# Causal attention and two feed-forward layers on one core: 128 stationary columns for every first score chunk, a minimum that moves rows to the other half of the partitions, and a new order of all operations

## The chip, the cores and the metric

One core of a Trainium2 chip runs the whole program in one launch. The metric is device time in microseconds of one execution, from the runs' times. Three runs of the kernel before took 589.15, 589.16 and 590.04 us, a median of 589.16 us. The profile is of one more execution: it took 589.2 us, of which 587.4 us lie between its first and its last instruction (the span). The other 1.8 us lie around the span. All positions below are microseconds from the span's start.

## The reference, cut to what matters

```
q, k, v: (2, 12, 448, 64) float32; scores = q @ k.T / 8, masked above the diagonal with -1e9
attn = exp(scores - max); attn = attn / (sum(attn) + 1e-9); x = attn @ v        # 24 heads
x -> (896, 768)                                       # tokens by 12 heads * 64
g = x @ w_gate; x = (g * sigmoid(g) * (x @ w_val)) @ w_out                      # d_ff 1536
h = x @ w_in; r = max(h, 0); out = (r * r) @ w_out2                             # d_ff 2048
```

The weights arrive as 64-bit floats. The kernel takes each weight tile as pairs of 32-bit words and splits it into two fp32r parts (whi, wlo). The activations are split in the same way (hi, lo), and each product is made of three matmuls.

## The kernel before

**The two stages.** The attention runs first, for 12 pairs of heads (p = 0 to 11; heads 2p and 2p+1). The feed-forward layers follow, a long row of matmuls in a fixed order (`products`, L880 and L1057). While the attention runs, the first two weight units are split (jobs J, L589 to L620), and one early product of the first unit (L880, tile early) fills two gaps near the end.

**One pair of heads, job by job.** Each job has a letter in the planner.

- LD loads q, k and v (SyncE's queue; for pair 0 also ScalarE's).
- AT turns q or k with four matmuls against the identity (L734). AC copies the result to SBUF (L740 on VectorE, L742 on ScalarE).
- S makes the scores of row chunk i of both heads (`score_mm`, L758). A head has 448 rows: chunk 0 has 64 rows and 64 columns, chunks 1, 2 and 3 have 128 rows and 192, 320 and 448 columns. The two heads lie on partitions 0 to 63 and 64 to 127 of the operand, so that two matmuls run side by side, in the two row halves of the array. Before, chunk 0 of the two heads is one 128x64 tile: each head's matmul has 64 stationary columns, and the second head's result is written to partitions 64 to 127 of the same PSUM bank.
- M takes the scaled and masked scores out of PSUM with VectorE and keeps each row's minimum (`score_max`, L775). E is the exponential with its sum (L781, ScalarE).
- RA adds 1e-9 to the sums (L786), R inverts them (L791, VectorE), N scales the rows (`normalise`, L808 or, on ScalarE, L806), NT moves 64 rows to the other partition half (`normalise_tail`, also through `scale_by`).
- T turns the probabilities, 8 matmuls for a head in two groups (L823 to L833). H copies a group out of PSUM (L843 VectorE, L845 ScalarE). V multiplies with the values, for a pair (L852). XH and XL split the result (L863, L868).

**What sets the order.** `attention_plan` gives every job an engine, a cost in ns, the jobs it waits for and the buffers it takes. `Plan.run` is a list scheduler: of all jobs that can start it takes the one that starts earliest, and among equals the one with the lowest rank (RANK plus a table FIRST with one entry per job). The jobs are then written out in that order, and each engine runs its own jobs in exactly that order. Tables in OPT choose the engine of each AC ("acd"), RA ("rad"), N ("n"), NT ("nt") and H ("h"). Where the plan sees TensorE idle in the first 24 us, `bank` writes idle matmuls (L522, `keep_warm`) into the gap; they run whether the gap is there or not. PSUM has 8 banks, taken in turn; a pair's scores take 4.

Of the kernel before, what the change touches and what calls it, by code (L numbers as in the profile page):

```python
# [10 lines left out]
F32 = mybir.dt.float32  # L11
# [342 lines left out]
def act_cost(n, sbuf=False, extra=0):  # L354
    return 76 + 0.833 * n + 43 * sbuf + 93 * extra
# [751 lines left out]
```

## Time and profile before

| | kernel before |
|---|---|
| median of 3 runs | 589.16 us (589.15 to 590.04) |
| profiled execution, its span | 589.2 us, 587.4 us |
| granted TensorE clock over the span | 1.000 |
| TensorE busy | 581.0 us (99%) |
| VectorE, ScalarE, GpSimd busy | 467.6, 283.9, 44.9 us |
| chain that ended last, by engine | PE 87%, DVE 4%, ACT 3%, DMA 2%, POOL 1% |

The engines are PE (TensorE's matmuls), PEld (its weight loads), DVE (VectorE), ACT (ScalarE), POOL (GpSimd) and SP (SyncE, which issues most DMAs). A line number is one of the kernel before. Matmuls are pipelined, so the records of neighbouring matmuls overlap, and a busy PE need not be a full one: what a group of matmuls costs is read from its start to the start of the next group.

### The profile page before, as it was taken

Reading aid. Unit: us, or ns where it says so; the run is one execution under the profiler, and the core shown is the slowest. Engines: PE = TensorE matmul, PEld = TensorE weight load, DVE = VectorE, ACT = ScalarE, POOL = GpSimd, SP = SyncE. Lnnn points to the kernel's source line nnn. Section 1 sums busy time; section 2 is a strip of 40 time slices with the busy share of each in tenths; the row PEclk is TensorE's granted clock in tenths of the full one; section 3 lists DMA queues with packets and bytes.
Section 4 is the critical chain, followed back from the end, with each engine's and each line's share of the span. In section 5 each row is a group of like instructions: output and inputs, shape, how many; then the busy total and the mean of one; then the engine's idle time right before and its main releaser. Section 6 shows DMA issues by size and latency. Waiting matters only on the chain.

```text
span 587.4 us, 8665 instructions
## 1 busy us (share of the span) xinstructions
PE 581.0 (99%) x3234; PEld 525.9 (90%) x3235; DVE 467.6 (80%) x851; ACT 283.9 (48%) x541; POOL 44.9 (8%) x119
## 2 busy tenths in 40 slices
PE   8999999999999999999999999999999999999997
PEld 4766678999999999999999999999999999999997
DVE  4998895998888888888777777888888897649741
ACT  5999895443333333332333335777777732223201
POOL 2555640000000000000000000000000000000000
PEclk9999999999999999999999999999999999999999
DMA  8775140343333333333333332333334343345102
GB/s 171 182 165 127 33 137 26 112 156 108 108 108 108 108 107 108 108 107 109 108 112 110 110 115 92 109 107 108 109 109 112 107 153 112 107 148 161 55 1 94
DMA packets 80777, 65.04 MB, mean 111 GB/s; under 512 B 34912, under 2 KB 76640, under 8 KB 80736
## 3 DMA queue, kind: packets, MB, share of 16 engines
q1 hardware_dynamic: 79808, 64.27, 37.1%
q8 instruction: 25, 0.41, 0.3%
q10 hardware_dynamic: 928, 0.23, 0.2%
q14 instruction: 16, 0.13, 0.1%
HBM read 61.73 MB, written 2.75 MB: 110 GB/s over the span
## 4 chain that ended last, share of the span: by engine, by line
PE 87%; DVE 4%; ACT 3%; DMA 2%; POOL 1%; SPq 1%; issue 1%; ACTq 0%; POOLq 0%
PE o L1057 20%; PE h L880 20%; PE v L880 15%; PE y L880 15%; PE g L880 14%; ACT P L781 2%; PE s L758 2%; POOL P L808 1%; DMA raw<-in_k_dram 1%; DVE P L775 1%; PE x L852 1%; DMA wraw<-in_moe_w_gate_dram 1%; DVE P L808 1%; DVE pt L843 1%; SPq L719 1%
## 5 line engine op out<-in xcount | busy, mean ns | idle before, releaser
L607 ACT ACTIVATE whi<-wa 128x768 fp32r<-128x768 f32 x68 | 57.4, 844 | 123.3 <-DVE wa L601 80.8
L1057 PE MATMUL o<-whi,b 128*128 128x384 f32 x336 | 85.5, 334 | 0.0
L880 PE MATMUL y<-b,whi 128*128 128x480 f32 (+1 forms) x288 | 69.2, 362 | 0.0
L589 ACT ACTIVATE wa<-wraw 128x768 f32<-128x768 f32 x68 | 61.7, 908 | 11.5 <-DVE wlo L620 11.1
L880 PE MATMUL h<-b,whi 128*128 128x480 f32 (+1 forms) x256 | 66.7, 362 | 0.0
L617 DVE TENSOR_TENSOR wa<-wa,whi 128x768 f32<-128x768 f32 x68 | 64.6, 950 | 0.4 <-ACT whi L607 0.4
L601 DVE SCALAR_TENSOR_TENSOR wa<-wraw,wa 128x768 uint32<-128x768 uint32 x68 | 64.7, 952 | 0.0
L614 DVE SCALAR_TENSOR_TENSOR wr<-wraw,wr 128x768 f32<-128x768 uint32 x68 | 64.7, 951 | 0.1
L620 DVE TENSOR_TENSOR wlo<-wa,wr 128x768 fp32r<-128x768 f32 x68 | 64.5, 949 | 0.1
L592 DVE TENSOR_SCALAR wa<-wa 128x768 f32<-128x768 f32 x68 | 38.0, 559 | 32.7 <-ACT wa L589 32.7
L1057 PEld LDWEIGHTS o<-whi,b 128*128 128x128 f32 x336 | 60.7, 188 | 0.0
L880 PEld LDWEIGHTS y<-b,whi 128*128 128x128 f32 x288 | 53.9, 187 | 3.7
L1057 PE MATMUL o<-wlo,b 128*128 128x384 f32 x168 | 56.1, 334 | 0.0
L880 PE MATMUL h<-b,wlo 128*128 128x480 f32 x192 | 53.9, 362 | 0.0
L880 PEld LDWEIGHTS h<-b,whi 128*128 128x128 f32 x256 | 48.0, 187 | 3.2
L967 ACT ACTIVATE b<-u 128x480 fp32r<-128x480 f32 (+2 forms) x24 | 13.9, 580 | 69.0 <-DVE u L963 69.0
L781 ACT ACTIVATE P<-P,st 128x448 f32<-128x448 f32 (+3 forms) x84 | 43.7, 523 | 3.1 <-DVE st L775 2.6
L880 PE MATMUL v<-ahi,whi 128*128 128x480 f32 (+2 forms) x144 | 40.4, 362 | 0.0
L880 PE MATMUL v<-alo,whi 128*128 128x480 f32 (+2 forms) x144 | 40.4, 362 | 0.0
L880 PE MATMUL v<-ahi,wlo 128*128 128x480 f32 (+2 forms) x144 | 40.4, 362 | 0.0
L880 PE MATMUL y<-b,wlo 128*128 128x480 f32 (+1 forms) x144 | 40.4, 362 | 0.0
L610 DVE TENSOR_SCALAR wr<-wa 128x768 uint32<-128x768 uint32 x68 | 38.0, 558 | 1.8
(94 smaller groups left out, 1041.4 us busy)
## 6 DMA issues: line engine op xcount, KB each, us to landing
wraw<-in_moe_w_out_dram SPq DMA_DIRECT2D x28, 768.0 KB, 4.4
wraw<-in_moe_w_in_dram SPq DMA_DIRECT2D x16, 768.0 KB, 4.7
wraw<-in_moe_w_gate_dram SPq DMA_DIRECT2D x12, 768.0 KB, 4.3
wraw<-in_moe_w_val_dram SPq DMA_DIRECT2D x12, 768.0 KB, 4.3
out_dram<-osb SPq DMA_DIRECT2D x14, 192.0 KB, 1.9
raw<-in_q_dram SPq DMA_DIRECT2D x23, 112.0 KB, 2.8
raw<-in_k_dram SPq DMA_DIRECT2D x23, 112.0 KB, 3.0
v<-in_v_dram SPq DMA_DIRECT2D x24, 96.0 KB, 2.6
```

Source lines behind the costliest of these rows:

```text
L589: nc.scalar.activation(out=af, in_=high.bitcast(F32), func=AF.Abs)
L592: engine.tensor_scalar(out=af, in0=af, scalar1=W_TINY, scalar2=W_HUGE, op0=ALU.max, op1=ALU.min)
L601: nc.vector.scalar_tensor_tensor(out=a, in0=high, scalar=0xC0000000, in1=a, op0=ALU.bitwise_and, op1=ALU.bitwise_or)
L607: nc.scalar.activation(out=split_t[n][0], in_=af, func=AF.Copy)
L610: nc.vector.tensor_scalar(out=r[0], in0=a, scalar1=0xFF800000, scalar2=None, op0=ALU.bitwise_and)
L614: nc.vector.scalar_tensor_tensor(out=rf, in0=low, scalar=2.0 ** -52, in1=rf, op0=ALU.mult, op1=ALU.mult)
L617: engine.tensor_tensor(out=af, in0=af, in1=split_t[n][0].bitcast(F32), op=ALU.subtract)
L620: engine.tensor_tensor(out=split_t[n][1], in0=af, in1=r[0].bitcast(F32), op=ALU.add)
L781: nc.scalar.activation(out=a, in_=a, func=AF.Exp, scale=-1.0, bias=st(0), accum_out=st(1))
L880: nc.tensor.matmul(out=pss[z][:, :cols], lhsT=w[p == 2][:, c], rhs=xs[k][p == 1][:, at:at + cols], start=first and k == 0 and p == 0, stop ...
L967: nc.scalar.activation(out=g_hi[m][:, at(c)], in_=up[z][:, :c[1]], func=AF.Copy)
L1057: nc.tensor.matmul(out=pss[t][:, :N], lhsT=a[f][:, tk], rhs=w[:, c], start=f + n == 0, stop=f == KF2 - 1 and n == 2)
```

## The change

Chunk 0 of the second head now takes 128 stationary columns, like every other chunk, and goes to a PSUM bank of its own. Only the first 64 rows of the result are used. Each head has an M job of its own for chunk 0 (64x64): the second head's reads PSUM partitions 0 to 63 and writes SBUF partitions 64 to 127, so that the exponential can still take both heads in one instruction. That one now waits for two M jobs. The second mask tile is gone. The planner's costs are new, FIRST is a new and shorter table, and a weight job on DVE with two tensor inputs now holds GpSimd in the plan. Nearly all engine choices go back to one default: AC on ACT, RA and N on POOL, NT on DVE, H group 0 on ACT and group 1 on DVE.

```diff
 FIRST = {
-    ('AC', 0, 0): -907.75, ('AC', 0, 1): 3963.19, ('AC', 1, 0): 2864.38, ('AC', 1, 1): -1686.58,
...
+    ('AC', 0, 0): 2.15, ('AC', 0, 1): 2.15, ('AC', 1, 0): 2.15, ('AC', 1, 1): 23.63,
...
-    "acd": ((0, 0), (2, 0), (5, 0), (11, 0), (11, 1)),
+    "acd": (),
-    "rad": (3, 5, 19, 20, 21, 22),
-    "pack": 1,
+    "rad": (),
+    "pack": 2,
...
+        (1, 3): 'D', (17, 2): 'D', (21, 2): 'D',
...
+            if k[0] == "J" and engine == "DVE" and k[2] in (3, 6, 7, 8):
+                free["Pool"] = max(free.get("Pool", 0), start) + cost
...
-    return 76 + 0.833 * n + 43 * sbuf + 93 * extra
+    return 51 + 0.833 * n
...
-    return 109 + 1.042 * n / wide
+    return 70 + 1.042 * n
...
-            ps = s_bank[p, z][e if i else 0][:, at:at + n]
+            x, ps = qk_s[p][64 * e:64 * e + 64], s_bank[p, z][e][:, at:at + n]
             nc.tensor.matmul(
-                out=ps if i else ps[64 * e:64 * e + 64], lhsT=x[:, 0, QE[i]:QE[i] + m],
-                rhs=x[:, 1, :n], start=True, stop=True)
-            sps[2 * p + (e if i else 0), i] = ps
+                out=ps, lhsT=x[:, 0, QE[i]:QE[i] + 128], rhs=x[:, 1, :n], start=True, stop=True)
+            sps[2 * p + e, i] = ps[:n - QE[i]]
...
     def score_max(h, i):
-        a, st = probs(h, i)
-        n = a.shape[1]
-        by = mask[:, S - n:] if i else mask2
+        a, st = probs(h, i, True)
+        rows, n = a.shape
+        end = S - 128 + rows
         nc.vector.tensor_tensor_reduce(
-            out=a, in0=sps.pop((h, i)), in1=by, scale=-SCALE,
+            out=a, in0=sps.pop((h, i)), in1=mask[:rows, end - n:end], scale=-SCALE,
             scalar=3.0e38, op0=ALU.add, op1=ALU.min, accum_out=st(0))
```

**The start, on TensorE.** Before, after the first warm-up matmuls and twelve turning matmuls (x12: q and k of pair 0, q of pair 1), the order is:

```order
L758 MATMUL s<-qk 128x448 x2
L758 MATMUL s<-qk 64x64 x2
L758 MATMUL s<-qk 128x320 x2
L758 MATMUL s<-qk 128x192 x2
L734 MATMUL qk<-ident,raw 128x112 x12
L758 MATMUL s<-qk 128x448 x2
L758 MATMUL s<-qk 64x64 x2
```

With the change, from the turning matmuls on (qk are turned queries and keys, s scores):

```order
L601 MATMUL qk<-ident,raw 128x112 x16
L624 MATMUL s<-qk 128x448 x2
L624 MATMUL s<-qk 128x64 x2
L624 MATMUL s<-qk 128x320 x2
L624 MATMUL s<-qk 128x192 x2
L624 MATMUL s<-qk 128x448 x2
L624 MATMUL s<-qk 128x64 x2
```

The first scores now stand behind k of pair 1 as well (16 instead of 12), and the second pair's scores follow at once, where before q and k of pair 2 stood between. From there to the first turned probabilities (T of head 0) the change has 8 turning matmuls, 5 idle ones, 4 turning, the scores of pair 2 and 4 idle ones. Before had the scores of pairs 1 and 2, 8 turning matmuls and 10 idle ones.

**Later, on TensorE**, about pair 5's scores and the values of pairs 2 and 3 (x). Before:

```order
L758 MATMUL s<-qk 128x448 x2
L852 MATMUL x<-pt,v 64x448 x2
L852 MATMUL x<-pt,v 64x320 x2
L758 MATMUL s<-qk 64x64 x2
L758 MATMUL s<-qk 128x320 x2
L758 MATMUL s<-qk 128x192 x2
L852 MATMUL x<-pt,v 64x192 x2
L852 MATMUL x<-pt,v 64x64 x2
```

and with the change:

```order
L718 MATMUL x<-pt,v 64x448 x2
L624 MATMUL s<-qk 128x448 x2
L624 MATMUL s<-qk 128x64 x2
L624 MATMUL s<-qk 128x320 x2
L624 MATMUL s<-qk 128x192 x2
L718 MATMUL x<-pt,v 64x320 x2
```

The four chunks of a pair's scores stay together in every pair with the change; before, some pairs were cut up, as this one.

## Rows read from the trace of the kernel before

**Rows 1.** Busy time of each engine, attention split at the first T.

```profile
core 0: us, PE busy (x) PEld busy (x) DVE busy (x) ACT busy (x) POOL busy (x), PEclk, DMA share, GB/s
0.00:19.02 19.02, 16.70 (x98) 9.06 (x100) 10.62 (x54) 11.79 (x36) 4.67 (x31) 1.00 0.78 163
19.02:96.33 77.31, 76.68 (x613) 53.18 (x612) 69.24 (x240) 69.95 (x208) 40.18 (x88) 1.00 0.47 120
```

**Rows 2.** Timeline of PE's start: start us, us, engine, line, what, [idle before].

```profile
6.07 0.57 PE L734 MATMUL qk<-ident,raw 112*128 112x112 f32 x4 [0.52 <-DMA raw<-in_q_dram]
6.57 2.35 PE L758 MATMUL s<-qk 64*128 64x448 f32 x16
...
10.52 0.57 PE L734 MATMUL qk<-ident,raw 112*128 112x112 f32 x4 [0.68 <-DMA raw<-in_k_dram]
...
16.61 2.56 PE L522 MATMUL pt<-const-bfloat16-1.0 128*128 128x512 bf16 x10 [0.25 <-ACT qk L742]
19.02 0.27 PE L823 MATMUL pt<-ident,P 128*128 128x128 f32 x1
```

**Rows 3.** Timeline of PE later: S, V, two T heads, AT, early, layer one.

```profile
21.07 2.35 PE L758 MATMUL s<-qk 64*128 64x448 f32 x16
23.35 1.95 PE L852 MATMUL x<-pt,v 128*64 128x448 f32 x16
25.23 0.33 PE L823 MATMUL pt<-ident,P 128*128 128x128 f32 x1
...
26.16 0.27 PE L823 MATMUL pt<-ident,P 128*128 128x128 f32 x1
...
27.03 0.93 PE L734 MATMUL qk<-ident,raw 112*128 112x112 f32 x8
...
44.62 2.08 PE L734 MATMUL qk<-ident,raw 112*128 112x112 f32 x20
46.63 1.02 PE L758 MATMUL s<-qk 64*128 64x448 f32 x4
...
94.71 0.36 PE L880 MATMUL early<-alo,whi 128*128 128x448 f32 x1
...
96.33 0.36 PE L880 MATMUL g<-ahi,whi 128*128 128x448 f32 x1
```

**Rows 4.** Timeline of PE inside the scores that begin at 21.07.

```profile
22.02 0.33 PE L758 MATMUL s<-qk 64*64 64x64 f32 x4
...
22.28 0.54 PE L758 MATMUL s<-qk 64*128 64x320 f32 x2
...
22.93 0.49 PE L758 MATMUL s<-qk 64*128 64x192 f32 x4
```

**Rows 5.** Timeline of SyncE's queue: issues of q and k of pair 1.

```profile
1.69 1.01 SPq L713 DMA_DIRECT2D raw<-in_q_dram  x2
2.75 1.02 SPq L713 DMA_DIRECT2D raw<-in_k_dram  x2
```

**Rows 6.** Groups, first 100 us: count, busy us, mean ns, idle before.

```profile
L775 DVE CUSTOM_DVE_ANT_0 P<-s,mask 128x64 f32<-128x64 f32 x12 | 2.6, 216 | 0.5 <-PE s L758 0.4
L808 DVE TENSOR_SCALAR P<-P,st 64x64 f32<-64x64 f32 x17 | 5.4, 318 | 1.3 <-POOL P L808 0.9
L808 DVE TENSOR_SCALAR P<-P,st 128x192 f32<-128x192 f32 x6 | 2.3, 375 | 0.0
L740 DVE COPY qk<-qk 128x448 f32<-128x448 f32 x5 | 3.1, 617 | 4.2 <-PE qk L734 3.9
L742 ACT ACTIVATE qk<-qk 128x448 f32<-128x448 f32 x19 | 9.6, 541 | 4.3 <-PE qk L734 4.3
L806 ACT ACTIVATE P<-P,st 64x64 f32<-64x64 f32 (+3 forms) x12 | 4.9, 429 | 0.9 <-POOL P L808 0.4 <-DVE st L791 0.4
L808 POOL TENSOR_SCALAR P<-P,st 128x448 f32<-128x448 f32 x17 | 11.8, 695 | 2.4 <-DVE st L791 2.0 <-POOL P L808 0.2
```

**Rows 7.** Timelines of DVE and POOL: one move of 64 rows beside GpSimd's work.

```profile
67.92 0.75 DVE L808 TENSOR_SCALAR P<-P,st 64x64 f32<-64x64 f32 x1 [0.95 <-POOL P L808]
...
66.29 2.33 POOL L808 TENSOR_SCALAR P<-P,st 128x448 f32<-128x448 f32 x4 [0.58 <-DVE st L791]
```

More of the change, by code (lines that the diff above doesn't have):

```diff
@@ L218 @@
     "rings": {'bank': 8, 'raw': 3, 'rawv': 5, 'sp': 4, 'P': 6, 'pt': 4, 'wraw': 3, 'wa': 2, 'wr': 1, 'ws': 3},
-    "ld0": ((1240, 2700), (510, 2700), (1020, 2700), (1020, 2700)),
-    "at0": 660,
-    "acd": ((0, 0), (2, 0), (5, 0), (11, 0), (11, 1)),
+    "ld0": ((1170, 2400), (520, 2450), (1050, 1900), (1050, 1950)),
+    "at0": 750,
+    "acd": (),
     "s0": (3, 0, 2, 1),
@@ L234 @@
         (0, 0): 'D', (0, 1): 'D', (0, 2): 'D', (0, 3): 'D', (1, 0): 'D', (1, 1): 'D', (1, 2): 'D',
[5 rows of a table removed]
+        (1, 3): 'D', (17, 2): 'D', (21, 2): 'D',
     },
     "h": {
-        (13, 1): 0, (14, 1): 0, (15, 0): 1, (16, 1): 0, (17, 1): 0, (18, 0): 1, (18, 1): 0,
-        (19, 0): 1, (20, 1): 0, (22, 0): 1, (22, 1): 0, (23, 0): 1, (23, 1): 0,
+        (17, 1): 0,
     },
     "nt": {
-        0: 'P', 3: 'P', 4: 'P', 5: 'P', 6: 'P', 7: 'A', 8: 'P', 9: 'P', 10: 'P', 12: 'P', 13: 'A',
-        15: 'A', 17: 'A', 19: 'P', 20: 'P', 21: 'P', 23: 'P',
     },
@@ L284, in add @@
     def add(self, key, engine, cost, after=(), takes=(), uses=(), rank=0, later=0, cols=0):
-        later += 200 if engine == "PE" else 120
+        later += 200 if engine == "PE" else 150
         rank += self.first.get(key, 0)
@@ L351, in run, with act_cost, dve_cost @@
         return sorted(order, key=lambda o: o[0]) if len(order) == len(ops) else None
-def act_cost(n, sbuf=False, extra=0):
-    return 76 + 0.833 * n + 43 * sbuf + 93 * extra
-def dve_cost(n, wide=1):
-    return 109 + 1.042 * n / wide
+def act_cost(n):
+    return 51 + 0.833 * n
+def dve_cost(n):
+    return 70 + 1.042 * n
 def scaling(engine, n):
-    return {"D": ("DVE", dve_cost(n, 2)), "P": ("Pool", 280 + 0.83 * n),
-            "A": ("ACT", act_cost(n, True))}[engine]
+    return {"D": ("DVE", 135 + 0.51 * n), "P": ("Pool", max(395, 245 + 0.83 * n)),
+            "A": ("ACT", 310 + 0.45 * n)}[engine]
 def attention_plan(NP, NPAIR, NC, S, U, KD, rank=RANK, opt=OPT):
@@ L377, in attention_plan @@
         for z in range(2):
-            cost, later = opt["ld0"][2 * p + z] if p < 2 else (1280, 1300)
+            cost, later = opt["ld0"][2 * p + z] if p < 2 else (1250, 1450)
             add(("LD", p, z), "SP", cost, [("LD", p, 0)] if z else
@@ L381, in attention_plan @@
                 [raw] if z else [], t + z / 10 - 99 * (not p), later)
-        add(("LD", p, 2), "SP", 1280, [("LD", min(p + 1, NP - 1), 1)], [rawv], [], t + 2.2, 1300)
+        add(("LD", p, 2), "SP", 1560, [("LD", min(p + 1, NP - 1), 1)], [rawv], [], t + 2.2, 1350)
         for z in range(2):
@@ L400, in attention_plan @@
             for z, i in enumerate(order):
-                if opt["pack"] and not i and h % 2:
+                pair = opt["pack"] and not i
+                n, bk = QE[i + 1], ("bank", "s", h, [i in both for both in SHARED].index(True))
+                add(("M", h, i), "DVE", dve_cost(n) + 25 * (pair and h > t), [("S", p, i)], [],
+                    [bk, ("P", t) if pair else P], h + rank["M"] + z / 10)
+                if pair and h > t:
                     continue
-                n, bk = QE[i + 1], ("bank", "s", h, [i in both for both in SHARED].index(True))
-                add(("M", h, i), "DVE", dve_cost(n), [("S", p, i)], [], [bk, P],
-                    h + rank["M"] + z / 10)
-                add(("E", h, i), "ACT", act_cost(n, True, 2), [("M", h, i)], [], [P],
+                add(("E", h, i), "ACT", act_cost(n) + 227,
+                    [("M", x, i) for x in ((t, t + 1) if pair else (h,))], [], [P],
                     h + rank["E"] + z / 10)
-            add(("RA", h), *(("DVE", 110) if h in opt["rad"] else ("Pool", 260)), [("E", h, i) for i in range(h % 2 * opt["pack"], NC)], [], [P], h + rank["RA"])
-            add(("R", h), "DVE", 110, [("RA", h)], [], [P], h + rank["R"])
+            add(("RA", h), *(("DVE", 75) if h in opt["rad"] else ("Pool", 300)), [("E", h, i) for i in range(int(h % 2 and opt["pack"] > 0), NC)], [], [P], h + rank["RA"])
+            add(("R", h), "DVE", 90, [("RA", h)], [], [P], h + rank["R"])
             for i in reversed(range(NC)):
@@ L439, in attention_plan @@
         raw, a, b, ws = ("wraw", n), ("wa", n), ("wr", n), ("ws", n)
-        add(("W", n), "SP", 2200, [("LD", n, 1)], [raw], [], rank["W"] + 2 * n, 2500)
+        add(("W", n), "SP", 2450, [("LD", n, 1)], [raw], [], rank["W"] + 2 * n, 2500)
         for z in range(9):
             engine, cost, takes, uses = (
-                ("ACT", 900, [a], [raw]), ("DVE", 640, [], [a]), ("DVE", 720, [], [a]),
-                ("DVE", 1200, [], [raw, a]), ("ACT", 810, [ws], [a]),
-                ("DVE", 640, [b], [a]), ("DVE", 1130, [], [raw, b]),
-                ("DVE", 1080, [], [a, ws]), ("DVE", 1100, [], [a, b, ws]))[z]
+                ("ACT", 830, [a], [raw]), ("DVE", 480, [], [a]), ("DVE", 600, [], [a]),
+                ("DVE", 1030, [], [raw, a]), ("ACT", 740, [ws], [a]),
+                ("DVE", 500, [b], [a]), ("DVE", 1060, [], [raw, b]),
+                ("DVE", 880, [], [a, ws]), ("DVE", 880, [], [a, b, ws]))[z]
             if (n, z) in opt["j"]:
@@ L532, in emit_consts @@
         )
-        nc.gpsimd.tensor_copy(out=mask2[:64], in_=mask[:64, S - 128:S - 64])
-        nc.gpsimd.tensor_copy(out=mask2[64:], in_=mask[64:, S - 64:])
     units = []
@@ L689, in tile_attention_moe_moe @@
     mask = st_p.tile([128, S], F32, tag="mask", name="mask")
-    mask2 = st_p.tile([128, 64], F32, tag="mask2", name="mask2")
     NP = B * NPAIR
@@ L752, in score_mm, with probs @@
             s_bank[p, z] = [bank("s") for e in range(2)]
-        n, m = QE[i + 1], 128 if i else QE[1]
+        n = QE[i + 1]
         at = 0 if i == SHARED[z][0] else QE[SHARED[z][0] + 1]
         for e in range(2):
-            x = qk_s[p][64 * e:64 * e + 64]
-            ps = s_bank[p, z][e if i else 0][:, at:at + n]
+            x, ps = qk_s[p][64 * e:64 * e + 64], s_bank[p, z][e][:, at:at + n]
             nc.tensor.matmul(
-                out=ps if i else ps[64 * e:64 * e + 64], lhsT=x[:, 0, QE[i]:QE[i] + m],
-                rhs=x[:, 1, :n], start=True, stop=True)
-            sps[2 * p + (e if i else 0), i] = ps
-    def probs(h, i, rows=slice(None)):
-        if i:
-            return p_t[h][:, POFF[i]:POFF[i] + QE[i + 1]], lambda z: r_t[h][:, z, i:i + 1]
-        h, n = 2 * (h // 2), QE[1]
-        return p_t[h][rows, :n], lambda z: r_t[h][rows, z, :1]
+                out=ps, lhsT=x[:, 0, QE[i]:QE[i] + 128], rhs=x[:, 1, :n], start=True, stop=True)
+            sps[2 * p + e, i] = ps[:n - QE[i]]
+    def probs(h, i, half=False):
+        rows = slice(None)
+        if i == 0:
+            if half:
+                rows = slice(64 * (h % 2), 64 * (h % 2) + 64)
+            h -= h % 2
+        return p_t[h][rows, POFF[i]:POFF[i] + QE[i + 1]], lambda z: r_t[h][rows, z, i:i + 1]
     def score_max(h, i):
-        a, st = probs(h, i)
-        n = a.shape[1]
-        by = mask[:, S - n:] if i else mask2
+        a, st = probs(h, i, True)
+        rows, n = a.shape
+        end = S - 128 + rows
         nc.vector.tensor_tensor_reduce(
-            out=a, in0=sps.pop((h, i)), in1=by, scale=-SCALE,
+            out=a, in0=sps.pop((h, i)), in1=mask[:rows, end - n:end], scale=-SCALE,
             scalar=3.0e38, op0=ALU.add, op1=ALU.min, accum_out=st(0))
@@ L793, in normalise @@
     def normalise(h, i):
-        e = h % 2
-        a, st = probs(h, i, slice(None) if i else slice(64 * e, 64 * e + 64))
+        a, st = probs(h, i, True)
         o = a
```

213 rows, old and new, of tables (FIRST, OPT) are left out of this document.

## Prediction, made before the changed kernel ran

> **What bounds the kernel now.** I read the busy times by window first. From the first turned probabilities (T of head 0, 19.02) to the first matmul of layer one (g, 96.33) TensorE is busy 76.7 of 77.3 us at a clock of 1.00, while VectorE has 69.2, ScalarE 70.0 and GpSimd 40.2 [rows 1]. Busy matmuls need not be full ones, so I read next what a group costs from start to start, in PE's timeline [rows 3]: a pair's scores S 21.07 to 23.35 = 2.28 us; its values V 23.35 to 25.23 = 1.88; one head's T 26.16 to 27.03 = 0.87; twenty turning matmuls AT 44.62 to 46.63, 0.10 each; eight early matmuls 94.71 to 96.33, 0.20 each. After 19.02 the kernel before has 24 heads of T, 9 pairs of S, 12 of V, 64 AT, 18 early and one idle matmul of 0.3. That makes 20.9 + 20.5 + 22.6 + 6.4 + 3.6 + 0.3 = 74.3 us. It took 77.3, so 3.0 us are stalls and cut groups. TensorE is the bound of the attention from 19.02 on, and a schedule can win only two things: an earlier first T, and those 3.0 us. Before 19.02 TensorE waits for loads (0.52 us for q at 6.07, 0.68 for k at 10.52) [rows 2] and runs ten idle matmuls from 16.61 on (2.4 us). The layers after g take 587.4 - 96.33 = 491.0 us, and the change does not touch them.
>
> **The change, part by part.**
>
> *The start.* Scores of pair 0 now stand behind k of pair 1. q of pair 1 lets TensorE go on at 6.07 [rows 2]; k's two issues begin 2.75 - 1.69 = 1.06 us after q's [rows 5], so I put k's landing at 7.1, an estimate from these rows. Four AT take 0.5 as at 6.07 to 6.57, and the scores begin at 7.6 where they began at 6.57. That loses 1.0 us for VectorE and ScalarE. In return pair 1's scores follow at once: 7.6 + 2 x 2.28 = 12.2. Then come 8 AT (0.8, their k was there at 10.52), 5 idle matmuls at 0.24 (1.2; the ten before took 2.4), 4 AT (0.4 to 0.5), pair 2's scores (2.28) and 4 idle ones (1.0): T of head 0 at 18.0, 1.0 us earlier than 19.02. Four AT fewer are done by then (28 for 32): 0.4 is owed. Net 0.6 us gained. Head 0's probabilities should not be later than that: VectorE's first minimum comes 1.0 us later than before, and before, T had ten idle matmuls ahead of it.
>
> *TensorE after the first T.* 24 T, 9 S, 12 V, 68 AT and 18 early: 20.9 + 20.5 + 22.6 + 6.8 + 3.6 = 74.4 us. Without a stall, g would begin at 18.0 + 74.4 = 92.4. With all the old stalls it would be 95.4. All S groups are whole now, and the planner's costs stand nearer to the rows than the old ones, but ScalarE and VectorE have not much room. I take half, 1.5 us.
>
> *128 stationary columns for chunk 0.* Inside one S the 64-column piece takes 22.02 to 22.28 = 0.26 us, the 320-column one 0.65, the 192-column one 0.42 [rows 4]; the 448-column one, from 21.07 to 22.02, takes 0.95 [rows 3]. The wide ones already have 128 stationary columns. Each 128 columns less take 0.30 and 0.23 off, so a piece of 64 columns would come to some 0.2 to 0.3. I take no change. The ends: 0.06 less for each of 12 pairs (-0.7 us), or as dear as the 192-column piece (12 x 0.16 = +1.9 us).
>
> *Twelve more minima.* 12 x 0.216 = 2.6 us on VectorE [rows 6], taking the 64-row form at the price of the 128-row one, since both stream 64 columns. That the rows go to the other partition half has a near row: NT does so, on VectorE, at 0.318. Each pair's chunk 0 exponential now waits for the second head's minimum, so guard, reciprocal and scaling of the first head start later. That is hidden as long as the heads' scaled rows lie ready before their T; if not, it is the no-gain rival below.
>
> *Engine choices.* VectorE: 9 more pieces of 64x64 (17 to 26) x 0.318 = +2.9, ten wider pieces fewer at 0.375 or more = -3.8, five AC copies fewer and two H copies more, net three at 0.617 = -1.9 [rows 6]. With the minima: -0.2, nothing. ScalarE: 5 AC copies more (5 x 0.541 = +2.7), all 12 scalings gone (-4.9), two H fewer: -2.2 before those two. GpSimd: 13 more scalings and 6 more guards, at most 19 x 0.695 = 13.2 us, against 77.3 - 40.2 = 37.1 us that it stands idle [rows 1, 6]. So no engine passes TensorE by its sum.
>
> *The end.* The last V is followed by nine early matmuls as before (1.8 us), and layer one's first matmuls need only finished tiles. No cost.
>
> **Sum.** g at 18.0 + 74.4 + 1.5 = 93.9 instead of 96.33: 2.4 us earlier. From the profiled execution, 589.2 (the median of the runs is 589.16, the same), that is **586.8 us**.
>
> **The rivals.**
>
> *The plan holds to the end (no stalls): 585.3.* g at 92.4, 3.9 us earlier. For it: TensorE's groups have the same length wherever I looked, so the plan knows its bound well. Against it: three engines at 90% that wait for each other in a fixed order seldom leave none.
>
> *No gain: 588.6.* Scaled rows come late from GpSimd. One head now needs a guard and four scalings there, in a row, and the first head of a pair starts them later. Between pair 5's scores and T of head 10 TensorE now has only three V pieces, three heads of T less a half, one V and four AT. If T waits there and again in later pairs, the 3.0 us of stalls are back and only the start's 0.6 is left. For it: GpSimd's share rises most. Against it: its 37 us of idle time.
>
> *Slower: 592.8.* Moving 64 rows on VectorE can wait for GpSimd. At 67.92 one NT took 0.75 us where the mean is 0.318, and it ended only as a row of four GpSimd scalings did (66.29 + 2.33 = 68.62) [rows 6, 7]. The change gives VectorE an NT for every head and GpSimd nearly all scalings. If each of the 22 NT after the start took 0.75, VectorE would have 22 x 0.43 = 9.5 us more. It stands idle 77.3 - 69.2 = 8.1 us of the old window, 6.9 of the shorter one; if half of that can take the waits, 6.0 us come on top of the forecast. It decides from a mean wait of 3.45 / 22 = 0.16 us beyond the mean of 0.318. Against it: that mean already holds the waits of today, beside a GpSimd that is half busy. The Trainium skill speaks for this rival: SBUF — State Buffer, § SBUF: two separate sides, says that VectorE and GpSimd share one pair of ports, which the first to start holds for its whole instruction while the other waits. The row at 67.92 agrees with it, the mean of 0.318 says that it is seldom that long.
>
> *Also faster: 585.4.* Two changes of the array's shape fall away in each S (64x128 to 64x64 and back). The nearest row of a change of shape: a head's T after V takes 25.23 to 26.16 = 0.93, after another T 0.87 [rows 3], 0.06 more. 24 changes at that price are 1.4 us less than the forecast. Against it: the 64-column piece lies on the line of the wider ones, which shows no such price [rows 4]. By the Trainium skill, TensorEngine Tiling (Array Packing), § Key Properties, a change of the tiling mode drains TensorE; by that rule the two changes would have to show, and rows 4 does not bear it out.
>
> **How the numbers follow.** A measurement of this kernel can tell about 0.2% (1.2 us) from no change: faster is below 588.0, slower above 590.3. Chances: forecast 0.45, plan holds 0.17, shape changes 0.08, no gain 0.18, slower 0.12. Faster: the first three less a tail of 0.03 in which more stalls stay, and 0.03 of the no-gain case, 0.70. Same: 0.03 and the other 0.15, 0.18. Slower: 0.12. The range of the likeliest case alone is 585.9 to 588.3. The whole range reaches from 585.2 (no stalls) to 590.0, past no gain together with three quarters of the dearer chunk 0 (588.6 + 1.4), and leaves out the slower rival and a gain beyond the stalls.
>
> **What would show it.** In the profile of the changed kernel: the first T at about 18.0; g at about 93.9; S still 2.28 us from start to start; busy time on VectorE as before, ScalarE some 2 us less, GpSimd up to 13 us more. PE's waits should name VectorE or GpSimd at few T. The forecast is wrong if S is longer than 2.4 us, if the first T comes after 19, if NT's mean on VectorE passes 0.48 us, or if the span after g is not 491.0 us.

## The result, and the profile after

| | kernel before | changed kernel |
|---|---|---|
| median of the runs | 589.6 us (4 runs, 589.15 to 591.76) | 596.26 us (4 runs, 595.44 to 596.47) |
| ratio to before, 95% interval | | 1.0103 (1.0075 to 1.0131) |
| profiled execution, its span | 589.2, 587.4 us | 596.45, 594.7 us |
| first T, first matmul of layer one (g) | 19.02, 96.33 | 19.91, 103.39 |
| from g to the end of the span | 491.0 us | 491.3 us |

The changed kernel is slower by 1.0%, where 586.8 us was forecast. All of it arises before g: 7.06 us, against 7.3 us of span. The runs of the kernel before lie far apart: the 79 that ran beside the experiments below took 588.8 to 592.2 us, 18 of them more than 591.

The busy times, split at the first T. The second line answers to the second line of [rows 1].

```profile
core 0: us, PE busy (x) PEld busy (x) DVE busy (x) ACT busy (x) POOL busy (x), PEclk, DMA share, GB/s
0.00:19.91 19.91, 18.54 (x93) 11.01 (x94) 8.76 (x49) 11.42 (x32) 4.45 (x29) 1.00 0.82 170
19.91:103.39 83.48, 75.63 (x615) 56.30 (x614) 74.97 (x259) 67.37 (x202) 48.02 (x107) 1.00 0.42 107
```

From the first T to g TensorE is busy 1.05 us less than before (75.63 for 76.68) and idle 7.85 us where it was idle 0.63 (length less busy time). With the first T 0.89 us later: 0.89 - 1.05 + 7.22 = 7.06.

What TensorE waited for in that stretch (us in total, times, longest us):

```profile
PE pt L689 <- DVE P L674: 7.1, 7, 2.4
PE s L624 <- ACT qk L609: 0.8, 1, 0.8
```

Nearly all of it is T waiting for NT on VectorE (L674 is `scale_by`, the helper that issues the scalings). The longest wait, on three engines: PE's timeline, then DVE's, then POOL's (start us, us, engine, line, what, [idle before]).

```profile
38.09 0.33 PE L689 MATMUL pt<-ident,P 128*128 128x128 f32 x1 [2.44 <-DVE P L674]
...
36.27 1.76 DVE L674 TENSOR_SCALAR P<-P,st 64x64 f32<-64x64 f32 x1
...
34.74 3.65 POOL L674 TENSOR_SCALAR P<-P,st 128x448 f32<-128x448 f32 x8 [1.18 <-PE pt L696]
...
36.22 0.31 POOL L674 TENSOR_SCALAR P<-P,st 64x64 f32<-64x64 f32 x1
36.50 0.63 POOL L674 TENSOR_SCALAR P<-P,st 128x448 f32<-128x448 f32 x1
37.12 0.47 POOL L674 TENSOR_SCALAR P<-P,st 128x256 f32<-128x256 f32 x1
37.57 0.42 POOL L674 TENSOR_SCALAR P<-P,st 128x192 f32<-128x192 f32 x1
38.08 0.32 POOL L674 TENSOR_SCALAR P<-P,st 64x64 f32<-64x64 f32 x1
```

An NT (0.25 us is the median of the 64x64 scalings on VectorE) stood from 36.27 to 38.03. GpSimd began a scaling 0.05 us before it, and three more followed without a gap; NT ended as the last of these did (37.99). It is the picture of [rows 7], more than twice as long. A second NT stood 1.61 us and made T wait 0.75 (64.77). These two make 3.2 of the 7.1 us. Ahead of the other five waits (0.29 to 1.16, 3.9 us in all) NT took 0.25 or 0.26 us, but came late. Two of them, PE's lines and then DVE's:

```profile
66.95 0.33 PE L689 MATMUL pt<-ident,P 128*128 128x128 f32 x1 [1.09 <-DVE P L674]
...
75.63 0.33 PE L689 MATMUL pt<-ident,P 128*128 128x128 f32 x1 [1.16 <-DVE P L674]
...
63.10 1.61 DVE L674 TENSOR_SCALAR P<-P,st 64x64 f32<-64x64 f32 x1
...
66.64 0.25 DVE L674 TENSOR_SCALAR P<-P,st 64x64 f32<-64x64 f32 x1
...
75.32 0.25 DVE L674 TENSOR_SCALAR P<-P,st 64x64 f32<-64x64 f32 x1
```

Both stand directly behind an unbroken row of minima on VectorE, and in the first case that row stands behind the NT that was held until 64.71. The groups that answer to [rows 6] (count, busy us, mean ns, idle before):

```profile
L642 DVE CUSTOM_DVE_ANT_0 P<-s,mask 64x64 f32<-64x64 f32 x24 | 5.1, 212 | 0.4
L674 DVE TENSOR_SCALAR P<-P,st 64x64 f32<-64x64 f32 x26 | 10.8, 417 | 2.0 <-POOL P L674 1.3
L674 POOL TENSOR_SCALAR P<-P,st 128x448 f32<-128x448 f32 x22 | 14.7, 669 | 15.9 <-DVE st L658 11.4 <-PE pt L696 2.2 <-PE pt L699 2.2
```

Two more things stand in PE's timeline. At the start the engine is slow, though the granted clock reads 1.00 there (first line of the busy times above):

```profile
4.04 2.02 PE L601 MATMUL qk<-ident,raw 112*128 112x112 f32 x8
6.21 0.98 PE L601 MATMUL qk<-ident,raw 112*128 112x112 f32 x4 [0.15 <-DMA raw<-in_q_dram]
7.49 0.98 PE L601 MATMUL qk<-ident,raw 112*128 112x112 f32 x4 [0.30 <-DMA raw<-in_k_dram]
8.40 6.25 PE L624 MATMUL s<-qk 64*128 64x448 f32 x32
14.58 0.99 PE L601 MATMUL qk<-ident,raw 112*128 112x112 f32 x8
```

The scores of two pairs take 6.18 us from start to start (8.40 to 14.58), and four AT 0.91 (7.49 to 8.40), where [rows 2] shows 0.50. Later, a pair's scores are shorter than before:

```profile
24.44 2.11 PE L624 MATMUL s<-qk 64*128 64x448 f32 x16
...
25.29 0.66 PE L624 MATMUL s<-qk 64*128 64x64 f32 x6
...
25.46 0.50 PE L624 MATMUL s<-qk 64*128 64x320 f32 x2
...
26.05 0.50 PE L624 MATMUL s<-qk 64*128 64x192 f32 x4
...
26.48 0.60 PE L718 MATMUL x<-pt,v 128*64 128x448 f32 x2
```

That is 2.04 us from S to V, for 2.28 in [rows 3]. Piece by piece it is 0.85, 0.17, 0.59 and 0.43 us, for 0.95, 0.26, 0.65 and 0.42.

### The profile page after: what moved, and what is told of

Same layout as the page of the kernel before. It is cut to its first block, busy times and chain, and to the rows that moved or that the text cites. A ratio compares the mean times of both kernels' runs of the same rounds, so it can differ in the third digit from the quotient of the medians.

```text
span 594.7 us, 8720 instructions
## 1 busy us (share of the span) xinstructions
PE 582.0 (98%) x3232; PEld 531.1 (89%) x3232; DVE 471.4 (79%) x865; ACT 280.9 (47%) x532; POOL 52.5 (9%) x136
## 4 chain that ended last, share of the span: by engine, by line
PE 89%; DVE 7%; issue 1%; POOL 1%; DMA 1%; SPq 0%; ACT 0%; ACTq 0%; POOLq 0%
PE o L923 20%; PE h L746 19%; PE v L746 15%; PE y L746 15%; PE g L746 14%; DVE P L642 3%; PE x L718 2%; PE s L624 2%; DVE P L674 2%; PE pt L696 1%; POOL P L674 1%; DMA raw<-in_k_dram 1%; PE early L746 1%; DVE pt L709 1%; PE qk L601 0%
## 5 line engine op out<-in xcount | busy, mean ns | idle before, releaser
L648 ACT ACTIVATE P<-P,st 128x320 f32<-128x320 f32 (+3 forms) x84 | 43.9, 528 | 9.5 <-DVE st L642 8.6
L642 DVE CUSTOM_DVE_ANT_0 P<-s,mask 128x448 f32<-128x448 f32 (+3 forms) x96 | 36.6, 414 | 13.3 <-issue 9.7
L674 POOL TENSOR_SCALAR P<-P,st 128x448 f32<-128x448 f32 (+3 forms) x86 | 41.2, 494 | 18.4 <-DVE st L658 11.4
```

The costliest lines, as they stand in the source:

```text
L642: nc.vector.tensor_tensor_reduce(out=a, in0=sps.pop((h, i)), in1=mask[:rows, end - n:end], scale=-SCALE, scalar=3.0e38, op0=ALU.add, op1=A ...
L648: nc.scalar.activation(out=a, in_=a, func=AF.Exp, scale=-1.0, bias=st(0), accum_out=st(1))
L674: (nc.vector if engine == "D" else nc.gpsimd).tensor_scalar(out=o, in0=a, scalar1=by, scalar2=1.0, op0=ALU.mult, op1=ALU.mult)
```

## Experiments

Three theories: (A) NT on VectorE waits for GpSimd's rows of scalings. (B) TensorE starts at half its pace, and the rest follows. (C) The order, or the twelve minima, are dear by themselves. Every ratio below is to the kernel before, run on the same chip beside it (its medians there: 589.7 to 589.9 us).

### The chunk-0 change alone, in the order of before

```diff
-            ps = s_bank[p, z][e if i else 0][:, at:at + n]
+            x, ps = qk_s[p][64 * e:64 * e + 64], s_bank[p, z][e][:, at:at + n]
             nc.tensor.matmul(
-                out=ps if i else ps[64 * e:64 * e + 64], lhsT=x[:, 0, QE[i]:QE[i] + m],
+                out=ps, lhsT=x[:, 0, QE[i]:QE[i] + 128], rhs=x[:, 1, :n], start=True, stop=True)
...
             work[key[0]](*key[1:])
+            if key[0] == "M" and key[1] % 2 == 0 and key[2] == 0:
+                score_max(key[1] + 1, 0)
```

> Order and engine choices of the kernel before; only chunk 0 takes 128 stationary columns per head and the second head's minimum, put right behind the first's, moves its rows. If the 0.24 us that a pair's scores lost (2.28 to 2.04 from S to V) come from this alone: S at 2.04, g 2 to 3 us earlier, 586.2 to 587.2. Rival, the twelve added minima and the waits of the exponentials eat it: S at 2.04 all the same, but new waits at T, 588.8 to 590.5. Third, the 2.04 belongs to the new order: S stays 2.28, 589.

Measured: 590.69 us, ratio 1.0015 (1.0000 to 1.0030). S takes 2.04 us (29.64 to 31.68 in its PE timeline), so the gain belongs to the shape and not to the order. The nine pairs behind the first T should gain 9 x 0.24 = 2.2 us; g comes 1.45 us later (97.78). VectorE's busy time from the first T to g is 71.22 us for 69.24. The rival fits, 0.2 us beyond its range: the minima would eat the gain. Two more kernels part the two.

### 128 columns with one minimum, and 64 columns with two

The first takes the new scores and lets the old M read the first head's bank for both heads; the second splits the old M into two of 64 rows.

```diff
-            sps[2 * p + (e if i else 0), i] = ps
+            sps[2 * p + e, i] = ps
```

```diff
+        for e in range(2):
+            r = slice(64 * e, 64 * e + 64)
+            a, st = probs(h, 0, r)
+            nc.vector.tensor_tensor_reduce(
+                out=a, in0=x[r], in1=mask2[r], scale=-SCALE,
+                scalar=3.0e38, op0=ALU.add, op1=ALU.min, accum_out=st(0))
```

> The kernel before with 128 stationary columns for chunk 0 but one minimum over the first head's bank for both heads; the second head's chunk 0 is left out of it, so its values aren't those of the reference, the instructions are as many as before. It has the shorter scores without the twelve minima. If the scores' 0.24 us are TensorE time that counts: 586.5 to 587.8 for 589.9. Rival, VectorE and the waits behind it bound the stretch, not TensorE: 589 to 590.5, as with the twelve minima (590.7).

> The kernel before with 64-column chunk 0, but its one minimum a pair split in two of 64 rows, one behind the other: twelve minima more and nothing else. If VectorE's 2.5 us more go to the end: 591.5 to 593. Rival, they are hidden beside TensorE, as the prediction put it: 589.4 to 590.3, and the added cost of the 128-column version came from somewhere else (the second bank, the move of the rows).

Measured: 589.01 us, ratio 0.9984 (0.9971 to 0.9997), and 591.28 us, ratio 1.0018 (1.0004 to 1.0032). By the ratios that is 0.9 us less and 1.1 us more (by the medians 0.7 and 1.6), and together nothing, against the 0.0015 of the run above: they add up within their intervals. The first is at the edge of its rival's range, the second between the two: 12 x 0.24 = 2.9 us of TensorE give back a third. On VectorE the minima take 2.6 us more (24 x 0.218 for 12 x 0.216), and the read that follows each of them (0.08 us) 0.9 more; of these 3.5 us about a third is lost at the end. Neither engine is the bound of this stretch alone.

### The old chunk 0 in the changed kernel

```diff
-            x, ps = qk_s[p][64 * e:64 * e + 64], s_bank[p, z][e][:, at:at + n]
+            ps = s_bank[p, z][e if i else 0][:, at:at + n]
...
+            if key[0] == "M" and key[1] % 2 and key[2] == 0:
+                continue
             work[key[0]](*key[1:])
```

> Order and engine choices of the changed kernel, but chunk 0 with 64 stationary columns and one minimum a pair, as before. If TensorE's own length still sets the end there: S at 2.28 again, 9 x 0.24 = 2.2 us later at g, 598.4 to 599.2. Rival, the waits of T for VectorE set the end, and they take up the difference (or shrink, with 12 minima of 0.2 us gone): 594.5 to 597.

Measured: 594.98 us, ratio 1.0074 (1.0051 to 1.0098), 1.3 us below the changed kernel, as the rival had it. TensorE is busy 76.96 us from the first T to g (1.33 more), and idle 4.64 us for 7.85: T's waits for NT fall from 7.1 to 4.1 us. Here, too, the twelve minima seem to cost more than the shorter scores bring; the intervals of the two kernels overlap, so the size is not settled.

### NT out of GpSimd's way

Order, engine and place of NT stay; the form of the instruction changes.

```diff
+        elif engine == "X":
+            nc.vector.tensor_scalar(
+                out=o, in0=a, scalar1=by, scalar2=None, op0=ALU.mult, op1=ALU.add,
+                accum_out=scr[:o.shape[0]])
```

> The changed kernel with every NT on VectorE in the form that also sums its row into a scratch column (a sum nobody reads): same engine, same place in the order, one short read of the sum more. Theory that NT waits for GpSimd's rows of scalings through the ports they share: no NT over 0.45 us, mean 0.25 to 0.35 for 0.417; T's waits for NT from 7.1 us to 3 or less; 591 to 594. Rival, T waits because the work reaches NT late in the new order, whatever NT itself takes: T's waits stay at 5 us or more, 595.5 to 597.5.

Measured: 591.81 us, ratio 1.0023 (1.0007 to 1.0039): 4.45 us of the loss gone by the medians, as theory A had it (T's waits are 3.3 us, for 3 or less). Its NT group in the trace (18 to 104 us; ns min/median/max) and PE's wait:

```profile
L681 DVE TENSOR_SCALAR_CACHE_REDUCE P<-P,st x23: 269/277/279, 18.4 to 92.0; 64x64 f32<-64x64 f32 x23
...
PE pt L700 <- DVE P L681: 3.3, 6, 0.8
```

Not one NT is longer than 0.28 us, and the longest wait of T is 0.8 us for 2.4, though GpSimd's row of eight scalings is still there (3.66 us from 33.41 on). By VectorE's time alone little is gained: 24 x (0.276 + 0.08) = 8.5 us for some 10.3. What counts is that no NT is held at the wrong moment. In this profile the first T, which waits for nothing in either kernel, comes 1.33 us earlier (18.58), and that isn't NT's doing; from there to g it takes 3.33 us less (80.15 for 83.48), with 3.44 us less idle time (4.41 for 7.85). So theory A is shown for some 3.4 us in the profiles. The six waits that are left (0.32 to 0.79 us) stand behind NT of 0.28 us that came late. The Trainium skill, SBUF — State Buffer, § Who interferes with whom, names this form of tensor_scalar as one that doesn't take the pair of ports that VectorE shares with GpSimd; these rows agree.

### The engines and the order apart

Two kernels: the order of the changed kernel with the engine tables of before ("n", "h", "nt", "rad", "acd"), and the order of before with those of the changed one. The third is the second with NT in the summing form.

```diff
+PLAN = dict(OPT)
+OPT.update({
...
+})
...
-        for start, cost, engine, key in attention_plan(NP, NPAIR, NC, S, U, KD).run():
+        for start, cost, engine, key in attention_plan(NP, NPAIR, NC, S, U, KD, opt=PLAN).run():
```

> The order of the changed kernel word for word, but scalings, NT, guards, head copies and q/k copies on the engines that they had before. If it is the move of nearly all scalings to GpSimd and of all NT to VectorE that costs: T's waits for NT go below 3 us, 590 to 593. If it is the order itself (the late start, and short distances from scores to T): 595 to 600, since the order was laid out for the other engines.

> The order of the kernel before word for word, 64-column chunk 0 and one minimum a pair, but scalings, NT, guards, head copies and q/k copies on the engines of the changed kernel. If NT on VectorE beside nearly all scalings on GpSimd is what costs, in any order: NT's mean over 0.38 us, T's waits for NT or the scalings of several us, 593 to 598. Rival, the engine choice is harmless where the order leaves room: 589 to 591.

> The order of the kernel before with the engines of the changed one (596.3), and every NT in the summing form. If the ports are what made the engine choice dear there: 3 to 5 us back, 591 to 593.5. Rival, in that order it is GpSimd's own rows of scalings that come late (T waited 2.3 us for GpSimd and 1.8 for VectorE), and NT's form changes little: 595 to 596.5.

Measured: 593.28 us, ratio 1.0054 (1.0036 to 1.0073); 596.31 us, ratio 1.0108 (1.0078 to 1.0137); 596.12 us, ratio 1.0094 (1.0064 to 1.0123). The first fell between its two expectations: T waits for NT on VectorE no more, but 2.0 us for GpSimd and 1.2 for ScalarE. The second shows that the engine tables alone, in an order that was laid out for others, cost as much as all of the change. Its NT took 0.359 us on average and T waited 2.5 us for GpSimd, 1.8 for VectorE. In the third T still waits 2.6 us for GpSimd and 1.1 for VectorE: NT's form is not the main reason there, and in the order of before GpSimd itself comes late. PE's timeline of the second kernel, near the end, with GpSimd's below:

```profile
93.14 0.30 PE L833 MATMUL pt<-ident,P 128*128 128x128 f32 x1 [1.01 <-DVE P L818]
95.20 1.54 PE L840 MATMUL pt<-ident,P 128*128 128x128 f32 x6 [1.76 <-POOL P L818]
...
91.90 3.65 POOL L818 TENSOR_SCALAR P<-P,st 128x192 f32<-128x192 f32 x8
```

The last two heads' eight scalings stand in one row on GpSimd, with T behind them; in the kernel before ScalarE took four of them (L806, 87.19 to 89.52) and VectorE one, and GpSimd's row was half as long (87.29 to 89.15). How much of the 6.6 us lies here isn't settled. In the profile of the second kernel the clock fell behind these waits:

```profile
94.00:95.00 1.00, 0.00 (x0) 0.00 (x0) 0.43 (x1) 0.00 (x0) 1.00 (x3) 0.81 0.00 0
95.00:96.00 1.00, 0.80 (x4) 0.80 (x5) 0.00 (x0) 0.00 (x0) 0.46 (x2) 0.50 0.00 0
```

It stayed at 0.50 until about 98.0, and the matmuls of T from 95.20 to the last V (98.34) took 3.14 us where the same ones took 1.79 in the third kernel (97.13 to 98.92). In the profile of the third the first T came at 21.68, after a slow start, which the second's did not have (18.60).

### The slow start

```diff
-        keep_warm(bank("idle"), 7)
+        keep_warm(bank("idle"), 12)
```

> The changed kernel with 12 idle matmuls at the start for 7. In the changed kernel the 32 score matmuls of pairs 0 and 1 took 6.2 us at half the clock. If TensorE was cold only because it stood too long between small turning matmuls: S of pairs 0 and 1 in 4.1 us, first T at 18 to 18.6 for 19.91, and the same 1.3 to 1.9 us at the end, 594.3 to 595. Rival, the start is covered by the five and four idle matmuls behind it and by VectorE, so the first T moves less than 0.5: 595.7 to 596.5.

> Both edits on the changed kernel: NT on VectorE in the summing form, and 12 idle matmuls at the start. With 12 alone the first T came 2.8 us earlier (17.10), but the stall of 2.44 us before the T of head 6 stayed, TensorE fell to half its clock behind it (0.50 from 38 to 40), and only 0.4 us was left at g. If the stall is what gave the early start back: no clock under 1.00 after the first T, first T at 17.1, g 1 to 1.5 us earlier than with NT off the port alone (98.73), 590.2 to 591. Rival, VectorE takes the early start back whatever the clock does: g within 0.4 of 98.7, 591.5 to 592.

Measured: 595.99 us, ratio 1.0091 (1.0058 to 1.0124), and 590.48 us, ratio 1.0009 (0.9998 to 1.0019). The "half the clock" of the expectation is the pace of the matmuls; the granted clock reads 1.00 there. In the profile of the run with NT in the summing form, which starts with the same instructions, it does read 0.50, from about 7.4 to 10.8:

```profile
8.00:9.00 1.00, 1.00 (x5) 0.53 (x6) 0.00 (x0) 0.55 (x1) 0.00 (x0) 0.50 0.87 189
```

With 12 idle matmuls the scores of two pairs take 3.88 us for 6.18, and the first T stands at 17.10 and 16.95. Alone that brings 0.3 us at the end, as the rival had it but not for its reason (the first T moved 2.8 us); with NT out of the way it brings 1.3 us by the medians (0.8 by the ratios, whose intervals overlap). A reason stands in the windows of the first kernel, around the T of head 6:

```profile
34.00:35.00 1.00, 0.00 (x0) 0.00 (x0) 0.96 (x2) 1.00 (x4) 1.00 (x3) 1.00 0.69 176
35.00:36.00 1.00, 0.00 (x0) 0.00 (x0) 1.00 (x2) 0.51 (x3) 1.00 (x3) 1.00 0.94 279
36.00:37.00 1.00, 0.88 (x8) 0.89 (x9) 1.00 (x3) 0.13 (x1) 0.33 (x2) 1.00 1.06 372
37.00:38.00 1.00, 1.00 (x10) 1.00 (x8) 1.00 (x3) 1.00 (x4) 0.00 (x0) 0.72 1.18 280
38.00:39.00 1.00, 1.00 (x4) 0.30 (x5) 0.27 (x2) 0.94 (x3) 0.56 (x2) 0.50 0.54 101
39.00:40.00 1.00, 1.00 (x6) 0.02 (x2) 0.00 (x0) 1.00 (x5) 1.00 (x3) 0.50 0.80 179
40.00:41.00 1.00, 1.00 (x6) 0.60 (x6) 0.00 (x0) 0.80 (x2) 0.66 (x3) 0.57 0.00 0
41.00:42.00 1.00, 1.00 (x12) 0.67 (x10) 0.38 (x1) 0.00 (x0) 0.00 (x0) 1.00 0.00 0
```

The columns are those of the first table; the clock is the third from the end. TensorE stood still for 2.44 us (T of head 6 at 36.12, waiting for NT); by the windows' means the clock fell from 2.4 to 1.2 GHz at about 37.4, when it was at work again, and rose at about 40.9. Eight AT, a V piece and a pair's scores took 1.6 us more than the same ones in the changed kernel's profile (37.05 to 42.43 = 5.38, for 39.02 to 42.82 = 3.80), and of a lead of 2.81 us at the first T 1.97 were left at that T (36.12 for 38.09) and 0.39 at the T behind the scores (43.56 for 43.95). So in this profile the stretch at the lower clock took back most of what the start gave, and the two losses are not independent. In the second kernel, without the stall, no window after the first T is under 1.00, and the start counts.

### What is left of the change

The two edits above with the old chunk 0; and the same without the nine idle matmuls that the plan puts between the first pairs.

```diff
-                if start < Warmth.FROM:
+                if start < 0:
```

> The two edits of the run above, and chunk 0 as before (64 stationary columns, one minimum a pair): what is left of the change is its order and its engine choices. If the three losses add up (NT beside GpSimd -4.4 us, twelve minima against shorter scores -1.3, start -1): 588.6 to 589.8, no worse than the kernel before. If they overlap (each frees the same wait): 590.5 to 592.

> The run before (three parts undone, 588.9) without the nine idle matmuls between the first pairs: five ahead of the q copy of pair 2 and four ahead of the first T. Head 0's NT was done at 15.1 and head 1's at 16.8, the four idle ones stood from 16.73 to 17.61. If they only delay: first T at 16.5 to 16.8 for 17.61, 587.8 to 588.3. Rival, what TensorE gains there it waits for later, since VectorE and ScalarE don't start earlier: 588.7 to 589.2. Third, TensorE falls to half its clock in the gaps they leave: 590 or more.

Measured: 588.87 us, ratio 0.9976 (0.9964 to 0.9988), and 588.67 us, ratio 0.9977 (0.9967 to 0.9988). The first is within the expectation that the losses add up. One after the other the steps are 4.45 (NT), 1.33 (start) and 1.61 us (chunk 0), 7.39 in all; each by itself in the changed kernel they were 4.45, 0.27 and 1.28, 6.00 in all. The later two bring more once NT is out of the way. Both kernels beat the changed one, and the kernel before by 0.24% and 0.23%. That is not the worth of the order and engine choices alone: both have the 12 idle matmuls and the summing NT as well, and no run gave these to the kernel before. The runs of the first lie between 588.69 and 588.96 us, those of the kernel before beside it between 588.92 and 591.69; from the lowest run to the lowest it is 0.2 us. In the profile the first T comes 1.41 us earlier than before (17.61) and g 0.70 (95.63): what is gained is gained at the start. From there TensorE is idle 1.21 us, and little is left to wait for:

```profile
PE s L635 <- ACT qk L619: 0.6, 1, 0.6
PE pt L704 <- DVE P L685: 0.5, 2, 0.2
```

Taking the nine idle matmuls out brings the first T from 17.61 to 16.51, and g not at all (95.73): the rival's case, with a time just below its range. The scores of pair 2 now wait 0.60 us for ScalarE's copy (14.16), and a later T 0.29 for VectorE (20.55).

## Why the prediction was wrong

**Where the 9.5 us are.** g was forecast at 93.9 and came at 103.39. The first T was 1.9 us late (19.91 for 18.0), TensorE's idle time behind it 6.35 us too long (7.85 for 1.5), its busy time 1.2 (75.63 for 74.4). So the sum failed at the waits.

**What is right.** The layers after g kept their 491.0 us (491.3). ScalarE fell by 2.6 us from the first T on (2.2 forecast), GpSimd rose by 7.8 (at most 13.2).

**"TensorE after the first T", 3.0 us of stalls that fall to 1.5: this step failed, and with the wrong sign.** [Rows 1] already had TensorE idle for only 77.31 - 76.68 = 0.63 us; in the other 2.4 of the 3.0 us TensorE was busy, by the prediction's own account in cut groups, and no shorter wait for another engine gives those back. A gain of 1.5 us was not there to be had: with three parts of the change undone TensorE is still busy 76.81 us, for a sum of 74.4. The idle time went to 7.85 us instead.

**"Engine choices", nothing: this is where the largest part of the 7.85 us came from.** The step summed busy times, in which no engine passed TensorE. VectorE, forecast as before, rose by 5.7 us (69.24 to 74.97); its 64x64 scalings went from 5.4 to 10.8 us, where 2.9 more were forecast. But the tables put every NT on VectorE beside rows of scalings on GpSimd. The slower rival named that mechanism and priced it at 6 us on top of the forecast; 4.45 us came back when only NT's form was changed (3.4 us of idle time in the profiles). It was given 0.12 for a wrong reason: it was made to hang on NT's mean ("from a mean wait of 3.45 / 22 = 0.16 us"), and the mean came to 0.417, only 0.10 above 0.318 and below the 0.48 that was to decide. Few NT waited (five of the 26 pieces took 0.57 us or more), but two of those stood right ahead of a T: one of 1.76 us made a stall of 2.44. The same tables alone cost 6.6 us in the order of before, there with GpSimd late more than NT.

**"Twelve more minima", hidden: failed.** They cost about 1.1 us by themselves in the order of before. The sum left out the read behind each minimum (0.08 us, 12 more). How the delay reaches T is not shown job by job; in the changed order NT came late behind rows of minima, and with NT in the summing form T's waits for it fall from 3.3 to 0.5 us once the old chunk 0 is back.

**"128 stationary columns", no change, and the rival of the shape changes.** S went to 2.04 us, below the lower end given for it. The rival with 0.08 probably had the mechanism, at half its size: 0.24 us for two changes of shape would be 0.12 each, for 0.06. No run parts the shape from the bank: before, the two heads' chunk 0 also shared a PSUM bank, and now each has its own. The argument against it, that the 64-column piece lies on the line of the wider ones, failed since most of the price lies on the neighbours: the 448-column piece ahead of it lost 0.10, the 64-column one 0.09, the 320-column one behind it 0.06. The Trainium skill, TensorEngine Tiling (Array Packing), § Key Properties, had it that a change of mode drains TensorE, and the time lost ahead of the piece agrees with that. That it is worth only some 0.9 us of 2.9 at the end was in neither case.

**"The start", first T at 18.0: 19.91.** Its sum took TensorE at the pace of [rows 2]. The scores began at 8.40 for 7.6 (k's four AT began at 7.49 for 7.1 and took 0.91 us for 0.5), and two pairs took 6.18 us for 4.56. With 12 idle matmuls the order does better than forecast: 17.10 and 16.95, or 17.61 with the old, longer chunk 0.

**The sum.** With its three losses undone, this order comes to 588.87 us: faster by 0.24% by the ratio, 0.8 us by the medians, where 0.41% (2.4 of 589.2 us) was forecast. How much of that the kernel before would have gained from 12 idle matmuls stays open.

## What to carry to other kernels

Read idle time off the bounding engine before you promise to take stalls away: length less busy time is the most that shorter waits can give back, and the rest has to come from the engine's own groups. A resource that two engines share is to be priced at the longest wait in front of the bounding engine, not at the mean: find which short instruction stands there beside a long row of the other engine's, and give it a form or an engine without that resource. Measure an early start together with the stalls behind it: in one profile the clock fell behind a long stall, and most of the lead was gone. And when undoing losses ends in a gain, give the same repairs to the kernel before, which wasn't done here.

## What the runs showed of the hardware

- A 64x64 tensor_scalar on VectorE can stand through a row of GpSimd instructions and not only one: NT stood while four went by (36.22 to 37.99), the longest of which took 0.63 us. The Trainium skill, SBUF — State Buffer, § SBUF: two separate sides, says that the one that starts first has the shared pair of ports for its whole instruction, while the other waits. Here three more GpSimd instructions began before the VectorE instruction ended. It isn't always so: with the engine tables alone an NT at 64.60 took 0.42 us in the middle of a row of five (63.94 to 66.31). The form that also sums its row took 0.269 to 0.279 us beside such rows.
- A pair's scores took 0.24 us longer with a 64x64 chunk 0 of both heads in one bank than with 64x128 in a bank for each, spread over the piece itself and its neighbours on both sides. If it is the two changes between 64x128 and 64x64, that is 0.12 us for each.
- The granted clock fell from 1.00 to 0.50 for some 3.4 us (37.4 to 40.9 by the windows' means), not in a stall of TensorE of 2.44 us but about 1.3 us after it had ended. The changed kernel's profile has the same stall (38.09) and no fall, so a stall does not always bring it. With the engine tables alone it fell at about 94.6, in a wait of TensorE, and rose at about 98.0, with TensorE at work from 95.20 on.
- With 7 idle matmuls at the start, the scores of the first two pairs took 5.2 to 6.3 us in the four profiled kernels that have the order of the changed one, with 12 idle ones 3.9 to 4.4 us in the four others (the longer scores of the old chunk 0 among both). In the order of before, with 7, the first pair's scores took 2.0 to 2.3 us in five of six profiles and 4.2 us in the sixth.
